# Local and strided attention into a routed FFN on one core: the routing sum a step later, row tiles a step or two earlier, buffer clearing and stores moved

## The chip, the cores and the metric

One core of one Trainium2 chip runs the whole program. The metric is the device time of one execution in microseconds. The median of three runs before the change is 591.56 us (589.87, 591.56 and 591.76).

## What is computed

Attention over 8 batches and 8 heads of 576 tokens with 64 features: the first four heads look back at most 31 tokens (Local), the other four at the tokens with the same position modulo 32 (Strided). The result, 4608 rows of 512 values, goes through a mixture of experts: every token is sent to the best of 8 experts, two matrix products with a ReLU between, scaled by the gate's probability.

```python
# attention, per batch and head
scores = scale * q @ k.T
mask = (rel >= 0) & (rel < 32)  if h < 4 else  (rel >= 0) & (key % 32 == query % 32)
attn = softmax(where(mask, scores, -1e9))
x[:, h*64:(h+1)*64] = attn @ v            # x: 4608 x 512

# mixture of experts
logits = x @ w_gate + modality_bias[modality_id]
e_idx  = argmax(logits, axis=1)
gate_w = softmax(logits)[e_idx]           # sum of exponents plus 1e-9
for e in range(8):
    t = e_idx == e
    out[t] = gate_w[t] * (relu(x[t] @ w1[e]) @ w2[e])
```

## The kernel before

The 8 batches are taken as 4 pairs. A pair has 8 units, four of two Local heads and four of two Strided heads in turn, 32 units in all. One loop runs over the units; each turn of it (a step) holds the scores s of a unit (L349), the turned exponents t (L219), the values o (L386) of an earlier unit, for the strided ones ss (L444), ts (L219) and ot (L494). This order on TensorE is written out by hand. VectorE, ScalarE and GpSimd get their order from a scheduler that keeps dependencies and a priority by position in the program; SP's queue is in the order of the program, with the loads of later units and stores between.

A strided unit's exponents are spread over four offsets by a masked multiply into the tile eb: two on VectorE (L479), two on ScalarE (L483). exs (L458, L459) are exponents before the division, enp (L465) after it.

When a pair ends (ends maps the number of its last unit to its buffers; three steps later), a generator finish_pair begins, which is advanced by one yield at each step. It transposes the pair's features: row tiles xs (strided features, from the buffers xcs to the rows xt, four transposes and one ScalarE copy, L511) and column tiles xl (L518), stores the rows xt to DRAM (xd), multiplies the gate (lg, ls) and then advances another generator, route, by its yields:
- lt turns the logits; lo is the logits less their maximum, its exponent is taken on ScalarE (L631); oh is the one-hot expert, cum its running count (L637).
- waits[1] steps later: sml, the sum of the exponents (L641, L642) and its reciprocal in val (L643), put behind the last enp (L465, list spots) by an ordering dependency without a wait (behind_units); then new, fst, stp and cnt (L645 to L651), the counts before each pair.
- waits[2] steps later: rk and po, the place of a token in its expert, cut into pos, paf and pbf; one-hots ha and hb (L672); hv (L681, GpSimd), the token and gate value times hb; waits[3] steps later the matmul en (L687), which turns the table ent and is stored to the list ld.
- tabulate, from the second pair on: the matmul ct (L735) sums cnt over the partitions, cts copies it, and a chain on VectorE (L746 to L836) makes the table of which expert fills which of 12 slots of 384 tokens.

The stores of the rows are not issued at once, but put on a list and issued one by one, some per step, by the table SPREAD; GpSimd issues those of pairs 0 and 1 (L581), SP those of pair 2 (L577), ScalarE those of pair 3 (L577). Three buffers raw for weights (1 MB each) are loaded on GpSimd by indirect DMA (L904); the third of them shares its memory with the rows of pair 2, and its load waits until their stores have landed. fx buffers (tokens gathered, L872) are cleared by ScalarE (L870) before the first gathers, in the first microseconds.

The FFN runs over the 12 slots: for each of 8 blocks 12 matmuls h (L1036) and 9 matmuls o (L1050), with weights split into a high and a low part by ScalarE (wh, L1071) and VectorE (wl, L1072), hh (L1039) and hl the split of h. Between, as far as it goes, stand the last steps of pair 3: its column and row tiles and its routing.

Of the kernel before, what the change touches and what calls it, by code (L numbers as in the profile page):

```python
# [11 lines left out]
F32 = mybir.dt.float32  # L12
# [8 lines left out]
P = 128  # L21
# [25 lines left out]
EARLY, BEGIN, HOLD = 3, 28, 26  # L47
SPREAD = 1, 2, 1, 0, 1, 1, 2, 1
ROWS = 32, 24
# [137 lines left out]
def attention_moe(ctx: ExitStack, tc: tile.TileContext, a, out):  # L187
# [7 lines left out]
    def pa(name):  # L195
        return ps.tile([P, 512], F32, tag="a", name=name)
# [64 lines left out]

    spots, exps = [], []

# [140 lines left out]
    class Strided:  # L404
# [63 lines left out]
        def turn(self):  # L468
            n, r0 = self.n, ROWS[self.n % 2]
            kn = r0 + 72  # L470
            tp = pa(f"ts{n}").rearrange("p (g q) -> p g q", g=4)
            for g in range(4):
                c0 = 32 + 72 * g
                self.point = turned_to(tp[0:kn, g, :], self.en[:, c0 - r0:c0 + 72])
            self.eb = eb = lp.tile([104, 8, 4, 36], F32, tag="eb", name=f"eb{n}")
            src = tp[0:kn].rearrange("p g (j x) -> p (g j) x", j=2)[:, :, 0:36]
            sh = [kn, 8, 2, 36]
            c0 = C_T + 4 * (n % 2)
            nc.vector.tensor_tensor(  # L479
                eb[0:kn, :, 0:2, :], src.unsqueeze(2).to_broadcast(sh),  # L480
                cf[0:kn, c0:c0 + 2].unsqueeze(1).unsqueeze(3).to_broadcast(sh), ALU.mult)
            for t in (2, 3):
                nc.scalar.activation(eb[0:kn, :, t, :], src, AF.Copy, scale=cf[0:kn, c0 + t:c0 + t + 1])  # L483

        def values(self):
            n, eb, vs, b = self.n, self.eb, vsp[self.n % 2], self.b
            kn = ROWS[n % 2] + 72
            for g2 in range(2):
# [13 lines left out]
                mark(nc.scalar.copy(dst, ot.rearrange("p (r q) -> p r q", r=16)))  # L502

    def finish_pair(bp, xt, xcs):

        def rows_of(c, k0):
            kn = min(4, 9 - k0)
            t = pa(f"xs{bp}{c}{k0}").rearrange("p (g q) -> p g q", g=4)
            for k in range(kn):
                turned_to(t[:, k, :], xcs[2 + c][:, P * (k0 + k):P * (k0 + k + 1)])  # L510
            nc.scalar.copy(xt[:, k0:k0 + kn, 256 + P * c:256 + P * c + P], t[:, :kn, :])  # L511

# [10 lines left out]

        if bp < EARLY:
            routing = route(bp, xt, xcs, (0, 1, 1, 1))
            next(routing)
            for c in range(2):
                rows_of(c, 0)
                columns_of(c, 0)
# [32 lines left out]
        next(routing)  # L562
        for k0 in (0, 4, 8):
            for c in range(2):
                next(routing, None)
                yield
                rows_of(c, k0)
            store_rows(bp, xt, k0, min(4, 9 - k0), nc.scalar)
        yield from routing
# [13 lines left out]
    def route(bp, xt, xcs, waits=(LT, RS, RK - RS, LW)):  # L583
# [56 lines left out]
        sm = ap.tile([P, 9], F32, tag="sml", name=f"sml{bp}")  # L640
        behind_units(nc.vector.tensor_reduce(sm[:], lo[:], AX.X, ALU.add))  # L641
        nc.vector.tensor_scalar(sm[:], sm[:], 1e-9, None, ALU.add)  # L642
# [27 lines left out]
        def hot(n, base, at, name, dt):  # L670
# [5 lines left out]

        ha = hot(LA, LA * bp, pa_f, "ha", F32)
        hb = hot(LB, 0, pb_f, "hb", BF16)
        hv = ap.tile([P, 9, 2, LB], F32, tag="hv", bufs=1, name=f"hv{bp}")
        sh = [P, 9, 2, LB]  # L680
        nc.gpsimd.tensor_tensor(  # L681
            hv[:], hb.unsqueeze(2).to_broadcast(sh), val.unsqueeze(3).to_broadcast(sh), ALU.mult)
        for _ in range(waits[3]):
            yield
# [179 lines left out]
    def token_parts(n, le, xrows):  # L864
# [3 lines left out]
        if n.startswith("0_"):  # L868
            for h in range(TH):
                nc.scalar.copy(xt[:, h, :], idle[:])  # L870
        for h in range(TH):
# [316 lines left out]
    for n in range(nu + 3):  # L1188
# [30 lines left out]
        if n + 2 < nu:  # L1219
            units[n + 2].prep()  # L1220
        ready = len(stores) if n >= HOLD else 9
        pop(POPS if n == nu + 2 else 1)
        for _ in range(min(ready, SPREAD[(n - 2) % 8])):
# [78 lines left out]
```

## Time and profile before

| | us |
|---|---|
| median of three runs | 591.56 |
| range of the runs | 589.87 to 591.76 |
| the profiled execution | 586.73 |
| span of it, first to last instruction | 584.7 |
| TensorE (PE) busy | 567.4 |
| VectorE (DVE) busy | 385.8 |
| ScalarE (ACT) busy | 331.4 |
| GpSimd (POOL) busy | 204.5 |

The attention phase lasts until about 150 us, the FFN from there to the end. PE is the queue of matmuls; idle time of the other engines counts only where PE waits for them. A row of the timeline gives the start in microseconds after the first instruction, the length, the engine, the line, the operation and its tiles, and in brackets how long the engine had stood still before and what ended that. Rows of one line that follow each other are drawn together (x64).

### The profile page before, as it was taken

Reading aid. Unit: us, or ns where it says so; the run is one execution under the profiler, and the core shown is the slowest. Engines: PE = TensorE matmul, PEld = TensorE weight load, DVE = VectorE, ACT = ScalarE, POOL = GpSimd, SP = SyncE. Lnnn points to the kernel's source line nnn. Section 1 sums busy time; section 2 is a strip of 40 time slices with the busy share of each in tenths; the row PEclk is TensorE's granted clock in tenths of the full one; section 3 lists DMA queues with packets and bytes.
Section 4 is the critical chain, followed back from the end, with each engine's and each line's share of the span. In section 5 each row is a group of like instructions: output and inputs, shape, how many; then the busy total and the mean of one; then the engine's idle time right before and its main releaser. Section 6 shows DMA issues by size and latency. Waiting matters only on the chain.

```text
span 584.7 us, 13778 instructions
## 1 busy us (share of the span) xinstructions
PE 567.4 (97%) x5449; PEld 500.9 (86%) x5449; DVE 385.8 (66%) x927; ACT 331.4 (57%) x662; POOL 204.5 (35%) x204
## 2 busy tenths in 40 slices
PE   9989999998999999999999999999999999999995
PEld 5878888777788899989999999989999998999984
DVE  6885977978866794676674756666574767664431
ACT  7789888787744454555453545545464455545342
POOL 3011021214257307444464335554433434423020
PEclk9999999999999999999999999999999999999998
DMA  8988889977796407766543275231413166323421
GB/s 274 342 283 267 296 289 302 307 253 233 259 357 222 191 1 242 248 200 223 150 161 73 80 208 198 59 83 63 91 54 81 50 219 201 112 42 126 145 103 46
DMA packets 63277, 104.31 MB, mean 178 GB/s; under 512 B 37027, under 2 KB 37539, under 8 KB 59108
## 3 DMA queue, kind: packets, MB, share of 16 engines
q0 software_dynamic: 16032, 57.47, 28.4%
q1 hardware_dynamic: 45636, 43.29, 25.4%
q10 hardware_dynamic: 1536, 2.58, 1.3%
q8 instruction: 45, 0.74, 0.5%
q14 instruction: 28, 0.23, 0.1%
HBM read 98.29 MB, written 19.18 MB: 201 GB/s over the span
## 4 chain that ended last, share of the span: by engine, by line
PE 86%; ACT 5%; DVE 5%; issue 3%; POOL 0%; DMA 0%; POOLq 0%; ACTq 0%; DVEq 0%
PE h L1036 35%; PE o L1050 34%; PE s L349 2%; PE ss L444 2%; PE o L386 2%; PE lg L589 1%; ACT et L373 1%; PE warm L207 1%; PE xl L219 1%; PE ot L494 1%; ACT xc L502 1%; PE t L219 1%; PE ts L219 1%; PE xs L219 1%; PE xt L219 1%
## 5 line engine op out<-in xcount | busy, mean ns | idle before, releaser
L1072 DVE TENSOR_TENSOR wl<-raw,wh 128x512 fp32r<-128x512 f32 x192 | 124.9, 688 | 83.8 <-ACT wh L1071 81.9
L1071 ACT CAST wh<-raw 128x512 fp32r<-128x512 f32 x192 | 109.7, 619 | 116.3 <-PE o L1050 110.3
L1036 PE MATMUL h<-xh,wl 128*128 128x384 f32 x384 | 129.7, 338 | 0.0
L1036 PE MATMUL h<-xl,wh 128*128 128x384 f32 x384 | 129.2, 336 | 0.0
L1036 PE MATMUL h<-xh,wh 128*128 128x384 f32 x384 | 128.1, 337 | 0.0
L1050 PE MATMUL o<-wl,hh 128*128 128x512 f32 x288 | 113.8, 395 | 0.0
L1050 PE MATMUL o<-wh,hl 128*128 128x512 f32 x288 | 113.7, 395 | 0.0
L1050 PE MATMUL o<-wh,hh 128*128 128x512 f32 x288 | 112.6, 391 | 0.0
L1039 ACT ACTIVATE hh<-h 128x384 fp32r<-128x384 f32 x96 | 47.2, 491 | 84.8 <-PE h L1036 84.3
L1041 DVE SCALAR_TENSOR_TENSOR hl<-h,hh 128x384 fp32r<-128x384 f32 x96 | 53.4, 556 | 55.4 <-ACT hh L1039 55.2
L904 POOL DMA_INDIRECT raw<-in_w,wi x48 | 55.8, 1162 | 83.2 <-ACT hh L1039 61.3
L1036 PEld LDWEIGHTS h<-xh,wh 128*128 128x128 f32 x384 | 72.2, 188 | 4.4 <-PE h L1036 0.4
L1036 PEld LDWEIGHTS h<-xl,wh 128*128 128x128 f32 x384 | 72.1, 188 | 4.0 <-issue 0.8
L1036 PEld LDWEIGHTS h<-xh,wl 128*128 128x128 f32 x384 | 72.0, 188 | 0.2 <-issue 0.2
L872 POOL DMA_INDIRECT fx<-xd,le x36 | 41.8, 1162 | 84.0 <-DMA work<-work 31.5
L1050 PEld LDWEIGHTS o<-wh,hl 128*128 128x128 f32 x288 | 54.0, 188 | 11.4
L1050 PEld LDWEIGHTS o<-wl,hh 128*128 128x128 f32 x288 | 54.0, 188 | 9.2
L1050 PEld LDWEIGHTS o<-wh,hh 128*128 128x128 f32 x288 | 54.1, 188 | 8.9
L889 POOL DMA_INDIRECT le<-ld,li x36 | 40.1, 1113 | 43.2 <-DVE li L811 15.8
L1058 POOL DMA_INDIRECT out<-y,le x36 | 37.0, 1027 | 38.5 <-ACT y L1057 34.5
L581 POOL DMA_DIRECT2D xd<-xt x18 | 10.0, 560 | 67.4 <-ACT xt L511 27.8
L999 DVE COPY work<-fx 128x1536 uint16<-128x1536 uint16 x18 | 30.7, 1745 | 3.1 <-DMA fx<-xd,le 3.1
(197 smaller groups left out, 768.7 us busy)
## 6 DMA issues: line engine op xcount, KB each, us to landing
vv<-in_vl SPq DMA_DIRECT2D x32, 292.5 KB, 4.4
qks<-in_qks SPq DMA_DIRECT2D x32, 288.0 KB, 4.6
qk<-in_qkl SPq DMA_DIRECT2D x16, 304.0 KB
qk<-in_qkl SPq DMA_DIRECT2D x16, 288.0 KB, 4.6
xd<-xt POOLq DMA_DIRECT2D x18, 256.0 KB, 5.1
vsp<-in_vs SPq DMA_DIRECT2D x16, 256.0 KB, 5.8
xd<-xt SPq DMA_DIRECT2D x9, 256.0 KB
xd<-xt ACTq DMA_DIRECT2D x2, 1024.0 KB, 6.6
```

Source lines behind the costliest of these rows:

```text
L219: return nc.tensor.transpose(dst, src, ident)
L872: ins = in_turn(nc.gpsimd.indirect_dma_start(xt[:, h, :], None, xd[0:xrows, :], IOA(ap=le[:, h, 0:1], axis=0), **bounds))
L889: in_turn(nc.gpsimd.indirect_dma_start(le[:, h, :], None, ld[0:1 + last, :], IOA(ap=li[:, s, h:h + 1], axis=0)))
L904: ins = nc.gpsimd.indirect_dma_start(raws[j].rearrange("p f c -> p (f c)"), None, a["w"], IOA(ap=wi[:, s, j:j + 1], axis=0), bounds_check= ...
L999: pin(nc.vector.tensor_copy(rows[:, :, w, :], halves(xt)[:, :, :, w]))
L1036: nc.tensor.matmul(hp, w[:, a1], x[:, c, :], start=(k == 0), stop=(k == 11))
L1039: steps.append(nc.scalar.activation(hh[:], hp, AF.Relu))
L1041: nc.vector.scalar_tensor_tensor(hl[:], hp, 0.0, hh.bitcast(F32), ALU.max, ALU.subtract)
L1050: nc.tensor.matmul(os[h], hx[:, m], w[:, 512:1024], start=(f == 0 and i == 0), stop=(f == 7 and i == 2))
L1058: outs.add(in_turn(nc.gpsimd.indirect_dma_start(out, IOA(ap=le[:, h, 0:1], axis=0), y[:], None, bounds_check=NT - 1, oob_is_err=False), True))
L1071: nc.scalar.copy(wh[:, c], raw[:, c])
L1072: nc.vector.tensor_tensor(wl[:, c], raw[:, c], wh[:, c].bitcast(F32), ALU.subtract)
```

## The change

- SPREAD, the table of stores per step, becomes 1, 2, 1, 0, 1, 2, 1, 1: the last entries are exchanged, so one store goes a step earlier.
- route is given (0, 2, 0, 1) steps for the first three pairs in place of (0, 1, 1, 1): sml, new, fst, stp and cnt come a step later, in the same step as rk; and sml is ordered behind the last masked multiply L479 (list ebs) instead of behind the last enp (list spots).
- turn_rows is rows_of moved out of finish_pair. The first row tile of each of the two feature blocks is done by the loop, one and two steps after the step of the pair's last unit; finish_pair begins three steps after it; for pair 3 this takes them out of the FFN's entry.
- In route, hb and hv stand ahead of ha in the program.
- The clearing copies of fx are tied to the last marked copy of the attention (pace), so that they come late in the attention phase, not at its start.
- Pair 3's rows are stored by SP's queue; the first store is issued when its generator starts.

```diff
-SPREAD = 1, 2, 1, 0, 1, 1, 2, 1
+SPREAD = 1, 2, 1, 0, 1, 2, 1, 1
...
-            nc.vector.tensor_tensor(
+            ebs.append(nc.vector.tensor_tensor(
                 eb[0:kn, :, 0:2, :], src.unsqueeze(2).to_broadcast(sh),
-                cf[0:kn, c0:c0 + 2].unsqueeze(1).unsqueeze(3).to_broadcast(sh), ALU.mult)
+                cf[0:kn, c0:c0 + 2].unsqueeze(1).unsqueeze(3).to_broadcast(sh), ALU.mult))
...
+    def turn_rows(bp, xt, xcs, c, k0):
+        kn = min(4, 9 - k0)
+        t = pa(f"xs{bp}{c}{k0}").rearrange("p (g q) -> p g q", g=4)
+        for k in range(kn):
+            turned_to(t[:, k, :], xcs[2 + c][:, P * (k0 + k):P * (k0 + k + 1)])
+        nc.scalar.copy(xt[:, k0:k0 + kn, 256 + P * c:256 + P * c + P], t[:, :kn, :])
...
-            routing = route(bp, xt, xcs, (0, 1, 1, 1))
+            routing = route(bp, xt, xcs, (0, 2, 0, 1))
             next(routing)
             for c in range(2):
-                rows_of(c, 0)
                 columns_of(c, 0)
...
-        for k0 in (0, 4, 8):
+        store_rows(bp, xt, 0, 4, nc.sync)
+        for k0 in (4, 8):
             for c in range(2):
                 next(routing, None)
                 yield
                 rows_of(c, k0)
-            store_rows(bp, xt, k0, min(4, 9 - k0), nc.scalar)
+            store_rows(bp, xt, k0, min(4, 9 - k0), nc.sync)
...
-        behind_units(nc.vector.tensor_reduce(sm[:], lo[:], AX.X, ALU.add))
+        behind_units(nc.vector.tensor_reduce(sm[:], lo[:], AX.X, ALU.add), ebs)
...
-        ha = hot(LA, LA * bp, pa_f, "ha", F32)
         hb = hot(LB, 0, pb_f, "hb", BF16)
...
         nc.gpsimd.tensor_tensor(
             hv[:], hb.unsqueeze(2).to_broadcast(sh), val.unsqueeze(3).to_broadcast(sh), ALU.mult)
+        ha = hot(LA, LA * bp, pa_f, "ha", F32)
...
-            nc.scalar.copy(xt[:, h, :], idle[:])
+            after_landing(nc.scalar.copy(xt[:, h, :], idle[:]), pace[-1])
...
+        if n - 1 in ends or n - 2 in ends:
+            turn_rows(*ends[n - 1 if n - 1 in ends else n - 2], 0 if n - 1 in ends else 1, 0)
```

On VectorE, in the routing of pair 1 as the units of pair 2 begin, the order before is this; sml and cnt are of the routing, mxs, eb and exs of a strided unit.

```order
L645 TENSOR_TENSOR new_2165<-cum_2086,ohb_2081 128x8
L646 TENSOR_TENSOR fst<-new_2165,cnt 128x8
L456 TENSOR_REDUCE mxs_2217<-ss_2136 128x16
L648 TENSOR_TENSOR stp<-fst 128x8
L651 TENSOR_TENSOR cnt<-cum_2086,fst 128x8
L641 TENSOR_REDUCE sml_2161<-lo_2068 128x9
L479 TENSOR_TENSOR eb_2233<-ts_2228,cf_sb 104x8x72
L458 TENSOR_TENSOR exs_2219<-ss_2136,mxs_2217 128x288
L642 TENSOR_SCALAR sml_2161<-sml_2161 128x9
```

In the same place the order after has eb first, and the counts are gone from here.

```order
L638 SCALAR_TENSOR_TENSOR cum_2086<-ohb_2081 128x72
L456 TENSOR_REDUCE mxs_2208<-ss_2136 128x16
L479 TENSOR_TENSOR eb_2224<-ts_2219,cf_sb 104x8x72
L642 TENSOR_REDUCE sml_2265<-lo_2068 128x9
L458 TENSOR_TENSOR exs_2210<-ss_2136,mxs_2208 128x288
```

The counts now stand some twenty operations further on, mixed with the last steps of the routing and with mx, ex and qd of a local unit. These are rows of the order after.

```order
L465 TENSOR_TENSOR enp_112<-exs_2210,sms_2213 128x288
L646 TENSOR_TENSOR new_2269<-cum_2086,ohb_2081 128x8
L669 SCALAR_TENSOR_TENSOR pbf_2287<-paf_2285,pos_2279 128x9
L673 TENSOR_TENSOR ha_2293<-cf_sb,paf_2285 128x324
L356 TENSOR_REDUCE mx_2299<-s_2232 128x5
L647 TENSOR_TENSOR fst<-new_2269,cnt 128x8
L673 TENSOR_TENSOR hb_2289<-cf_sb,pbf_2287 128x288
L359 TENSOR_TENSOR ex_2300<-s_2232,mx_2299 128x320
L330 COPY qd_102<-qk_2174 64x18x32
L649 TENSOR_TENSOR stp<-fst 128x8
L652 TENSOR_TENSOR cnt<-cum_2086,fst 128x8
L747 TENSOR_SCALAR ni_2377<-cts_2373 128x8
```

cnt, which stood ahead of sml, is now the last before ni, the first operation of the slot table.

On TensorE the matmul ct, which reads cnt and stp, stands in that step between the strided values ot and the strided scores ss; this is the order before.

```order
L494 MATMUL ot_2340<-eb_2233,vsp_113 64x72 x8
L494 MATMUL ot_2350<-eb_2233,vsp_113 64x72 x8
L735 LDWEIGHTS cb_sb
L735 MATMUL ct_2363<-cnt,cb_sb 128x16
L735 LDWEIGHTS cb_sb
L735 MATMUL ct_2363<-stp,cb_sb 128x16
L444 MATMUL ss_2338<-qks_2094,qz_104 36x18 x32
L219 MATMUL ts_2438<-cf_sb,enp_112 96x128 x4
L338 LDWEIGHTS cb_sb
L338 MATMUL s_2449<-cb_sb 128x256
```

In the order after a row tile xs stands ahead of it.

```order
L494 MATMUL ot_2341<-eb_2224,vsp_113 64x72 x8
L494 MATMUL ot_2351<-eb_2224,vsp_113 64x72 x8
L219 MATMUL xs_2364<-cf_sb,xc_136 128x128 x4
L736 LDWEIGHTS cb_sb
L736 MATMUL ct_2370<-cnt,cb_sb 128x16
L736 LDWEIGHTS cb_sb
L736 MATMUL ct_2370<-stp,cb_sb 128x16
L444 MATMUL ss_2339<-qks_2094,qz_104 36x18 x32
L219 MATMUL ts_2444<-cf_sb,enp_112 96x128 x4
L338 LDWEIGHTS cb_sb
```

The four transposes of xs have come in between; what comes behind ct is the same.

On ScalarE at the FFN's entry, the casts wh of the weights, the copies of column and row tiles (xc, xt) and the split hh of the first block stand like this before; wh_04 is the first to read the third weight buffer.

```order
L1071 CAST wh_02_3523<-raw_3157 128x512
L518 COPY xc_140<-xl_3431 128x512
L1071 CAST wh_02_3523<-raw_3157 128x512
L518 COPY xc_140<-xl_3437 128x128
L1071 CAST wh_03_3590<-raw_3157 128x512 x2
L511 COPY xt_138<-xs_3463 128x4x128
L1039 ACTIVATE hh_00_3427<-h_00_3414 128x384
L511 COPY xt_138<-xs_3501 128x4x128
L1071 CAST wh_04_3626<-raw_3224 128x512 x2
L577 DMA xd<-xt_138 128x4x512
L597 COPY ls_3461<-lg_3440 128x384
```

After, hh of the first block stands behind the casts of wh_04.

```order
L1072 CAST wh_02_3530<-raw_3158 128x512 x2
L1072 CAST wh_03_3590<-raw_3158 128x512 x2
L519 COPY xc_140<-xl_3443 128x512
L519 COPY xc_140<-xl_3449 128x128
L1072 CAST wh_04_3626<-raw_3230 128x512 x2
L1040 ACTIVATE hh_00_3439<-h_00_3426 128x384
L509 COPY xt_138<-xs_3476 128x4x128
```

The store of rows has left this queue.

## Rows read from the trace of the kernel before

**Rows 1.** The page: busy time, share of the span, instructions

```profile
span 584.7 us, 13778 instructions
PE 567.4 (97%) x5449; PEld 500.9 (86%) x5449; DVE 385.8 (66%) x927; ACT 331.4 (57%) x662; POOL 204.5 (35%) x204
```

**Rows 2.** Windows: length, busy of PE, PEld, DVE, ACT, POOL; clock, DMA share, GB/s

```profile
66.00:84.00 18.00, 16.49 (x402) 14.21 (x398) 14.19 (x54) 14.75 (x36) 4.08 (x7) 1.00 0.92 313
100.00:122.00 22.00, 19.54 (x492) 16.89 (x489) 19.95 (x100) 18.44 (x43) 4.09 (x7) 1.00 0.86 280
134.00:165.00 31.00, 29.00 (x406) 23.69 (x402) 25.51 (x111) 22.80 (x54) 12.59 (x13) 0.94 0.77 265
165.00:570.00 405.00, 405.00 (x2075) 366.79 (x2074) 252.70 (x430) 195.05 (x353) 168.13 (x150) 1.00 0.45 140
```

**Rows 3.** Timeline of PE: start, length, line, tiles, [idle before <-releaser], attention's end steps

```profile
41.46 0.34 PE L349 MATMUL s<-qk,qd 128*64 128x64 f32 x4 [2.00 <-issue]
...
106.77 0.18 PE L735 MATMUL ct<-cnt,cb_sb 128*128 128x16 bf16 x1
...
111.95 1.20 PE L687 MATMUL en<-hv,ha 128*36 128x64 f32 x18 [0.51 <-POOL hv L681]
...
116.62 0.66 PE L219 MATMUL xs<-cf_sb,xc 128*128 128x128 f32 x4 [0.43 <-ACT et L373]
...
119.99 0.25 PE L444 MATMUL ss<-qks,qz 128*36 128x18 f32 x5 [1.09 <-issue]
...
141.79 1.22 PE L494 MATMUL ot<-eb,vsp 104*64 104x72 f32 x32 [1.14 <-ACT eb L483]
...
144.01 0.63 PE L219 MATMUL ts<-cf_sb,enp 128*96 128x128 f32 x2 [0.86 <-DVE pbf L668]
```

**Rows 4.** Waits over the whole span: total, times, longest

```profile
DVE sml L641 <- ACT lo L631: 3.1, 3, 1.2
```

**Rows 5.** Timeline of DVE, the second pair's routing

```profile
101.80 0.16 DVE L651 TENSOR_TENSOR cnt<-cum,fst 128x8 bf16<-128x8 bf16 x1
103.12 0.23 DVE L641 TENSOR_REDUCE sml<-lo 128x9 f32<-128x72 f32 x1 [1.17 <-ACT lo L631]
103.26 0.75 DVE L479 TENSOR_TENSOR eb<-ts,cf_sb 104x576 f32<-104x576 f32 x1
...
107.72 0.46 DVE L465 TENSOR_TENSOR enp<-exs,sms 128x288 f32<-128x288 f32 x1
...
110.28 0.17 DVE L746 TENSOR_SCALAR ni<-cts 128x8 int32<-128x8 f32 x1
```

**Rows 6.** Timeline of ACT, the second and third pair's routing

```profile
102.81 0.27 ACT L631 ACTIVATE lo<-lo 128x72 f32<-128x72 f32 x1
...
134.80 1.19 ACT L373 COPY et<-t 64x512 f32<-64x512 f32 x2 [0.88 <-PE t L219]
...
140.85 0.89 ACT L483 ACTIVATE eb<-ts,cf_sb 104x288 f32<-104x288 f32 x2 [1.35 <-DVE eb L479]
```

**Rows 7.** Timeline of POOL: two stores, the value table, the third weight load

```profile
73.62 1.07 POOL L581 DMA_DIRECT2D xd<-xt  x2 [2.25 <-ACT xc L502]
74.70 1.17 POOL L681 TENSOR_TENSOR hv<-hb,val 128x576 f32<-128x576 bf16 x1
...
156.30 1.10 POOL L904 DMA_INDIRECT raw<-in_w,wi  x1 [9.29 <-ACT xc L518]
```

**Rows 8.** Timeline of ACT at the start: the clearing casts

```profile
2.56 3.20 ACT L870 CAST fx<-idle 128x512 f32<-128x512 bf16 x6
...
8.84 0.42 ACT L360 ACTIVATE ex<-ex 128x256 f32<-128x256 f32 x1 [1.81 <-DVE ex L359]
```

**Rows 9.** Timeline of ACT at the entry of the FFN

```profile
158.29 0.55 ACT L1039 ACTIVATE hh<-h 128x384 fp32r<-128x384 f32 x1
...
162.19 0.62 ACT L1071 CAST wh<-raw 128x512 fp32r<-128x512 f32 x1 [2.88 <-DMA raw<-in_w,wi]
```

**Rows 10.** Windows of 1 us, columns as in rows 2

```profile
144.00:145.00 1.00, 0.98 (x4) 0.63 (x4) 0.50 (x3) 0.83 (x3) 0.69 (x2) 0.50 1.03 405
```

More of the change, by code (lines that the diff above doesn't have):

```diff
@@ L260, in attention_moe @@
     stp = cp.tile([P, NBP, E], BF16, name="stp")
-    spots, exps = [], []
+    spots, exps, ebs = [], [], []
     def behind_units(ins, of=None):
@@ L502, in values @@
                 mark(nc.scalar.copy(dst, ot.rearrange("p (r q) -> p r q", r=16)))
-    def finish_pair(bp, xt, xcs):
[L506 to L511, printed above, removed]
+    def turn_rows(bp, xt, xcs, c, k0):
[4 more added lines that the diff above has]
+        nc.scalar.copy(xt[:, k0:k0 + kn, 256 + P * c:256 + P * c + P], t[:, :kn, :])
+    def finish_pair(bp, xt, xcs):
+        rows_of = partial(turn_rows, bp, xt, xcs)
         def columns_of(c, k0):
```

## The prediction, made before the changed kernel ran

> **What bounds the kernel now.** I read the page first: TensorE is busy for 567.4 of 584.7 us [rows 1], so no other engine is a bound on the whole, and a change can only bring back TensorE's idle time, or the time in which its clock is low, or add to these. The windows then say where that is. From 165 to 570 us TensorE is busy in all of 405.00 us [rows 2], and the change touches nothing there. Its idle time lies in the attention phase: 1.51 us in 66 to 84, 2.46 us in 100 to 122, 2.00 us in 134 to 165 (length less busy, [rows 2]); the last of these stretches also has a mean clock of 0.94 where the others have 1.00. The timeline of TensorE names what each gap waits for [rows 3]: the value table hv (0.51), a row tile's bank (0.43), the strided exponents eb (1.14), the chain behind pbf (0.86), and two gaps of 2.00 and 1.09 us that wait for nothing the profile shows. Last come the timelines of the engines that feed it. VectorE stands still in front of the routing sum sml, 3.1 us in three times [rows 4], and the next pair's masked-exponent multiply eb, and with it ScalarE's half of the same tile, stands behind it [rows 5, 6].
>
> A difference of 0.3% (1.8 us) is about what a measurement of this kernel can tell from none. The profiled execution took 586.73 us, 2.03 more than its span, and lies 4.83 below the median of the three runs, 591.56. I work out a difference against the profiled execution and lay it on the median.
>
> **The end of pair 0 (34 to 46 us).** Two row tiles of four transposes each (0.66 us, the length of the xs row in [rows 3], an upper bound since the next matmuls begin before its end) move from the pair's last step to one and two steps earlier. PE's work is the same; only what falls into idle time is gained. The first of them stands in front of the strided scores, the second in front of the local ones, in whose middle lies the 2.00 us gap [rows 3]. If that gap begins when it began, work ahead of it fills it; if it moves with the instructions, nothing is won. Bounds 0 and -1.3, I take **-0.6**.
>
> **Pair 0's routing under pair 1's end (66 to 84 us).** In the order after, eb runs before sml, during the time VectorE stood still, and sml follows when lo is there. The row of pair 1's routing shows the size: sml waits 1.17 us until ScalarE ends lo at 103.08 (102.81 + 0.27), and eb (0.75) comes after it [rows 5, 6]. So everything behind eb gains about 0.7; the exponents' subtraction exs still waits for sml. Further, hv on GpSimd stands behind two store issues, 1.07 us for both [rows 7]; with the new spread of stores one is left, and hv begins about 0.5 earlier, which closes the gap before en. All of this stretch's idle time is 1.51, and no more can be had. VectorE is nearly full here in steps, so the whole can't be counted on. Bounds -0.4 (the store alone) and -1.5, I take **-1.2**.
>
> **Pair 1's routing under pair 2 (100 to 122 us).** The same gain of 0.7 begins this stretch, but here a wait comes in that the kernel before doesn't have. The count matmul ct reads cnt. Before, cnt is done at 101.96 (101.80 + 0.16) while sml waits anyway, and ct runs at 106.77 without waiting [rows 3, 5]. Now new, fst, stp and cnt come behind the masked multiply enp, mixed with six operations (pbf, ha, mx, hb, ex, qd) which before fill the 2.56 us from enp's start at 107.72 to ni's at 110.28 [rows 5]. Four more small operations at a spacing of about 0.1 put cnt's end at 110.28 + 0.4, less 0.7 for the earlier eb: about 110.0. TensorE reaches ct at 106.77 + 0.66 for the row tile that now stands in front of it, 107.43, so it stands still for about 2.6 us; queued behind ct on its engine are the strided scores, enp's transposes, the outputs and the next scores, all of pair 2. Two waits further on are swallowed: 0.51 before en and 0.43 before a row tile [rows 3]. That leaves +1.6. Below, the 1.09 gap could be swallowed as well, and VectorE could drain half a microsecond sooner: 0. Above, +2.6, if none of the waits is. VectorE is the engine that decides, and it is busy for 19.95 of 22.00 us here [rows 2], so I stay with the working: **+1.5**.
>
> **Pair 2's routing and the entry of the FFN (134 to 165 us).** eb gains as before; ScalarE then sets ot's wait, because three clearing casts of 0.53 (3.20 / 6, [rows 8]) now stand in front of its et copies. 0.88 of their 1.6 us falls in ScalarE's idle time at 134.80, the rest in the 1.35 it waits at 140.85 [rows 6]. The 1.14 gap at ot shrinks to about 0.4. Then ct waits for cnt behind enp as above; since pbf, which TensorE waited for until 144.01 [rows 3], is just ahead of cnt on VectorE, ts moves by only +0.2. The first row tile falls in that wait and the second lands in the stretch that it was already in; taken out of the FFN's entry, the first is worth -0.5. What is open is the clock. After 1.14 and 0.86 us of idle time with 1.2 us of work between, it stands at 0.50 [rows 10]; a mean of 0.94 over 31 us is 0.06 x 31 / 0.5 = 3.7 us at half, 1.9 us of full-speed work lost [rows 2]. The two waits get somewhat shorter together (0.4 and about 1.3, in place of 2.00), so I count a quarter of this, -0.5. Sum of the stretch **-0.8**, bounds -2.5 (no fall of the clock) and +1.5 (the rival on the third weight load, below).
>
> By the Trainium skill (TensorE: Matmul & The Clock Gate, section "What's actually happening"), "the default state is throttled, and activity releases the throttle". This agrees with the 0.50 behind the two waits in [rows 10], and the 1.09 us gap in a stretch at 1.00 [rows 2, 3] shows that not every wait costs the clock; taken strictly, for any wait above that, the rule would make the ct wait of pair 1 cost the clock too, and that is the second rival.
>
> **What costs nothing.** The clearing casts at the start leave a ScalarE that, 2 us on, waits 1.81 us for VectorE [rows 8]: 0. One-hot hb ahead of ha in the code doesn't turn the two round on VectorE, where ha still comes first: 0 beyond the small move that I counted with hv. Pair 3's stores go to SP's queue and leave ScalarE's; they run earlier, beside a DMA that is busy for 0.77 of the stretch [rows 2], and nothing that TensorE wants is queued behind them on SP: 0, bounds -0.3 and +0.5. The masked exponents' spread on SP puts two stores instead of one ahead of the last unit's strided values; 0, and +0.5 if a store's rows are late.
>
> By the Trainium skill (DMA: Bandwidth & Descriptors, section "Issuing engines are not separate DMA queues"), a transfer issued from another engine runs on the same 16 DMA engines and saves only issue time. That speaks against a gain from the stores' new queue, and no run here shows it yet; the sum is the same with it, and the rival below on the third weight load would be the likelier for it.
>
> **Sum.** -0.6 - 1.2 + 1.5 - 0.8 = -1.1: 585.6 for a profiled execution, **590.5** on the median, -0.2%.
>
> **Rivals.**
> *The gains come whole and ct's wait is short.* For it: the wait in front of sml is real in three places, and each small operation behind enp is only 0.1 to 0.2 us. Against it: eight operations stand between enp and the end of cnt, and TensorE has nothing else queued. With -0.9, -1.5, +0.4 and -1.7 (no fall of the clock behind pair 2) the sum is -3.7: 587.9.
> *The ct wait costs the clock (the slower side).* A wait of 2.6 us in one piece in front of ct is longer than the 2.00 us in two that came before the clock of 0.50 [rows 3, 10]. If the clock falls there too, 1.9 us of work is lost, and with VectorE late the term is +2.6 in place of +1.5: -1.1 + 1.9 + 1.1 = +1.9, 593.5. It decides from where ct waits for more than about 2 us. Against it: the single wait of 2.00 us at 41.46 [rows 3] lies among work that went on as before.
> *The third weight load lands late.* Before, its issue on GpSimd waits 9.29 us, to 156.30 [rows 7], for pair 2's stores to land (it shares their buffer), and ScalarE has its data at 162.19; the first hh was done by then, at 158.29 [rows 9]. In the order after, the first hh stands behind the two casts of that load, so it can't start before it lands. With the same landing, hh0 would begin at about 163.4, five us later, and the first o group, due at about 165, slips by an estimated 0.7. For each microsecond by which it lands later, TensorE loses one. Against it: the stores are one fewer at the end, and should land earlier. With a landing 3 us later: -1.1 + 0.7 + 3 = +2.6, 594.2.
> *The change does nothing*, since DMA is nearly full (0.92 and 0.86 of the time, [rows 2]) and the loads set the pace: 0, 591.6. This is within the forecast's class.
>
> **How the numbers follow.** The sum, with the last rival in its class: 0.46, all of it within 0.3%. Whole gains: 0.34, faster. Clock: 0.14, slower. Third load: 0.06, slower. So faster by over 0.3% 0.34, within 0.3% 0.46, slower 0.20. The range of the forecast alone is 589.3 to 592.5, the sum with half of each bound. To hold eight in ten it must take in most of the whole gains and a part of the clock's case: 587.6 to 593.6.
>
> **What would show each step.** Right: VectorE's wait at sml under 0.9 us or gone in favour of a wait at exs, eb ahead of it, and TensorE's 1.14 gap at ot cut to under 0.5; a wait at ct of 2 to 3 us in pair 1 with cnt as its releaser; the gap before en gone in both pairs; a mean clock in 134 to 165 about as before. Wrong: ct not waiting (then the whole gains), a granted clock of 0.50 at 107 to 114 (then the second rival), hh0 later than 163 with TensorE waiting for it (the third), or a difference that arises behind 165, of which I know no reason.

## The result and the profile after

| | us |
|---|---|
| before, median of four runs | 590.71 |
| after, median of four runs (594.93 to 595.11) | 595.04 |
| ratio, 95% interval | 1.0074, 1.0049 to 1.0099 |
| profiled execution after, span | 595.11, 593.2 |

The change makes the kernel slower by 0.74%, some 4.3 us. The two profiled executions differ by 8.4 us, about twice that. The first one of before was short: a second trace of the same kernel, taken later, has 591.67 us and a span of 589.7. So size is read from the timed runs, and the place from the traces.

The windows of the kernel after (the columns of [rows 2]):

```profile
66.00:84.00 18.00, 17.32 (x398) 14.79 (x394) 15.56 (x54) 15.05 (x34) 4.17 (x7) 1.00 0.94 312
...
100.00:122.00 22.00, 17.96 (x394) 15.48 (x392) 18.73 (x94) 13.46 (x34) 4.22 (x7) 0.84 0.78 253
...
134.00:165.00 31.00, 26.74 (x432) 22.32 (x432) 25.13 (x116) 22.94 (x53) 10.22 (x11) 0.94 0.75 242
...
200.00:570.00 370.00, 370.00 (x1884) 335.44 (x1883) 232.42 (x379) 178.01 (x317) 144.46 (x130) 1.00 0.44 133
```

The same windows of the second trace of the kernel before:

```profile
66.00:84.00 18.00, 16.48 (x402) 14.20 (x399) 14.38 (x53) 14.73 (x36) 4.08 (x7) 1.00 0.92 312
100.00:122.00 22.00, 21.02 (x491) 17.98 (x486) 20.29 (x103) 18.48 (x44) 4.08 (x7) 1.00 0.88 300
134.00:165.00 31.00, 26.24 (x397) 20.49 (x394) 25.49 (x114) 21.97 (x52) 12.78 (x13) 1.00 0.72 247
```

From 200 to 570 us nothing has changed (all of 370.00 busy, as before). In 66 to 84 TensorE's idle time is 0.68 us where [rows 2] gave 1.51. The loss is in 100 to 122: 4.04 us idle (22.00 less 17.96) against 2.46 and 0.98 in the two traces before, and the mean clock is 0.84 where it was 1.00. In 134 to 165 it is 4.26 us, against 2.00 and 4.76; here the kernel before varies as much as the change does.

The timeline of TensorE after, beside [rows 3]:

```profile
105.26 0.66 PE L219 MATMUL xs<-cf_sb,xc 128*128 128x128 f32 x4
109.64 0.20 PE L736 MATMUL ct<-cnt,cb_sb 128*128 128x16 bf16 x1 [3.73 <-DVE cnt L652]
...
109.79 2.12 PE L444 MATMUL ss<-qks,qz 128*36 128x18 f32 x64
...
116.80 1.17 PE L688 MATMUL en<-hv,ha 128*36 128x64 f32 x18
...
147.94 0.66 PE L219 MATMUL xs<-cf_sb,xc 128*128 128x128 f32 x4
151.07 0.19 PE L736 MATMUL ct<-cnt,cb_sb 128*128 128x24 bf16 x1 [2.48 <-DVE hb L673]
```

ct, which didn't wait before, waits 3.73 us in pair 1, and 2.48 us in pair 2 (there the profile names hb; cnt is the second operation behind it on VectorE and ends 0.17 later, at 151.01). TensorE comes to it at 105.91 (109.64 less 3.73), 0.86 ahead of its time before, and to en at 116.80, 4.85 behind. The scores ss take 2.12 us behind the wait. In the trace of the kernel before they took 1.30:

```profile
107.07 1.30 PE L444 MATMUL ss<-qks,qz 128*36 128x18 f32 x64
```

The clock says why (windows of 1 us of the kernel after):

```profile
108.00:109.00 1.00, 0.00 (x0) 0.00 (x0) 1.00 (x2) 0.95 (x4) 0.98 (x2) 0.50 1.02 397
...
113.00:114.00 1.00, 1.00 (x14) 0.66 (x14) 1.00 (x3) 0.63 (x2) 0.00 (x0) 0.50 0.86 285
114.00:115.00 1.00, 1.00 (x30) 1.00 (x26) 0.99 (x7) 0.97 (x3) 0.00 (x0) 0.68 0.63 150
```

It is at 0.50 while TensorE still stands, and through the work behind the wait until 114.

VectorE and GpSimd in the same place, beside [rows 5] and [rows 7] (timelines, first VectorE, then GpSimd):

```profile
101.61 0.23 DVE L642 TENSOR_REDUCE sml<-lo 128x9 f32<-128x72 f32 x1 [0.80 <-ACT lo L632]
...
105.55 0.46 DVE L465 TENSOR_TENSOR enp<-exs,sms 128x288 f32<-128x288 f32 x1
...
107.73 0.45 DVE L330 COPY qd<-qk 64x576 f32<-64x576 f32 x1
108.09 1.41 DVE L649 TENSOR_TENSOR stp<-fst 128x8 bf16<-128x8 bf16 x1
109.43 0.15 DVE L652 TENSOR_TENSOR cnt<-cum,fst 128x8 bf16<-128x8 bf16 x1
```

```profile
104.73 1.07 POOL L582 DMA_DIRECT2D xd<-xt  x2 [2.65 <-DVE xt L399]
107.62 0.67 POOL L582 DMA_DIRECT2D xd<-xt  x1 [1.82 <-DVE hb L673]
108.31 1.17 POOL L681 TENSOR_TENSOR hv<-hb,val 128x576 f32<-128x576 bf16 x1
```

sml still waits 0.80 us, but eb no longer stands behind it. cnt is the last of the operations behind enp, and one of them, stp, takes 1.41 us. It runs beside hv on GpSimd and ends at 109.50, when hv does (108.31 + 1.17). In the trace of the kernel before it took 0.15:

```profile
101.73 0.15 DVE L648 TENSOR_TENSOR stp<-fst 128x8 bf16<-128x8 bf16 x1
```

### The profile page after: what moved, and what is told of

Read it like the earlier page. It is cut to its first block, busy times and chain, and to the rows that moved or that the text cites. A ratio compares the mean times of both kernels' runs of the same rounds, so it can differ in the third digit from the quotient of the medians.

```text
span 593.2 us, 13778 instructions
## 1 busy us (share of the span) xinstructions
PE 571.2 (96%) x5449; PEld 503.4 (85%) x5449; DVE 389.4 (66%) x927; ACT 331.2 (56%) x662; POOL 201.7 (34%) x204
## 4 chain that ended last, share of the span: by engine, by line
PE 80%; DVE 8%; issue 6%; ACT 3%; another core or an unknown queue 1%; POOL 0%; POOLq 0%; ACTq 0%
PE h L1037 33%; PE o L1051 32%; PE ss L444 2%; PE s L349 2%; PE o L386 2%; PE ot L494 1%; PE warm L207 1%; PE t L219 1%; PE lg L590 1%; DVE xt L399 1%; PE ts L219 1%; DVE mx L356 1%; PE xs L219 1%; PE xl L219 1%
## 5 line engine op out<-in xcount | busy, mean ns | idle before, releaser
L873 POOL DMA_INDIRECT fx<-xd,le x36 | 37.9, 1052 | 83.2 <-DMA work<-work 31.5
```

The lines of the kernel that those rows point to most:

```text
L873: ins = in_turn(nc.gpsimd.indirect_dma_start(xt[:, h, :], None, xd[0:xrows, :], IOA(ap=le[:, h, 0:1], axis=0), **bounds))
```

## The experiments

Two theories stood against each other. **A**: the counts stand behind the masked multiply enp on VectorE, ct on TensorE waits for them with all of pair 2 queued behind, and the clock falls. **B**: the row tiles, the clears or the stores cost the time. The kernels were timed in four groups, each on a chip of its own, with the kernel before beside them. Its median was 590.74 us in the first group (the first three kernels of the table), 591.29 in the second (the old table of stores, counts behind eb, ct a step later, row tiles alone), 585.92 in the third (the three with 583 to 586 us) and 589.92 in the fourth (the matmuls and the two repeated), so I compare ratios; times in an expectation are those of an earlier group or of the result.

| kernel | median us | ratio to before, 95% |
|---|---|---|
| counts a step earlier | 588.23 | 0.9962, 0.9933 to 0.9991 |
| the sum's edit alone | 597.65 | 1.0129, 1.0090 to 1.0168 |
| all but the sum's edit | 588.87 | 0.9966, 0.9938 to 0.9995 |
| the old table of stores | 593.05 | 1.0048, 1.0017 to 1.0079 |
| counts ordered behind eb | 587.10 | 0.9943, 0.9903 to 0.9983 |
| the same, again | 587.82 | 0.9972, 0.9944 to 1.0001 |
| ct a step later in pair 1 | 590.15 | 0.9975, 0.9952 to 0.9999 |
| row tiles alone | 589.64 | 0.9969, 0.9948 to 0.9990 |
| behind eb, stores on ScalarE's queue | 583.45 | 0.9951, 0.9932 to 0.9970 |
| behind eb, clears at the start | 583.79 | 0.9963, 0.9935 to 0.9991 |
| sum and counts behind eb, alone | 586.34 | 1.0019, 0.9990 to 1.0047 |
| matmuls in ct's wait | 591.17 | 1.0022, 0.9997 to 1.0047 |
| the change, again | 593.77 | 1.0075, 1.0051 to 1.0100 |

**A second trace of the kernel before.**

> The kernel before, unchanged, for a second trace. The first profiled execution (586.73 us) lies 2.7 to 5 us under the four timed runs (589.42 to 591.76). If those differ by where the clock falls or by waits in the attention phase, a profiled execution of about 590 shows 3 to 4 us more idle time or half-clock time there, and none behind 165 us. If the first trace is the usual course, this one has its gaps (sums of TensorE idle: 1.5 us in 66 to 84, 2.5 in 100 to 122, 2.0 in 134 to 165) within 0.5 us.

591.67 us. Its windows stand above. Idle time in 100 to 122 is less than in the first trace, in 134 to 165 it is 2.8 us more, for the most part because ot waits 1.6 for eb in place of 1.14, and h waits 1.6 for wh, which it didn't in the first. The entry of the FFN is where these two traces of the kernel before differ most; its time varies from 587.55 to 594.97 in 19 runs on this chip. Part of the expectation missed: 1.5 us more is idle behind 165 too, nearly all of it in one wait of h for xl (1.4, at 188.20).

**The counts put back.**

```diff
-        for _ in range(waits[1]):
+        for w in range(waits[1]):
             yield
+            if bp < EARLY and w == 0:
+                counts()
```

> The changed kernel, with new, fst, stp and cnt put back to one step before the routing sum (as in the kernel before), everything else as changed. Theory A (the count matmul ct waits for cnt behind the masked multiply, and the clock falls after the wait): ct does not wait in either pair, the half clock at 108 to 114 us is gone, and the time is 6 to 9 us under the changed kernel's 595.04, that is 586 to 589, under the kernel before by 2 to 4 us. Theory B (the row tiles, clears and stores cost the time): within 1.5 us of 595.04.

588.23 us, 0.38% under the kernel before. ct doesn't wait, and the clock in 100 to 122 is 1.00. Theory A holds, B is out.

**The sum's edit alone**, in the kernel before (waits 0, 2, 0, 1; sml behind ebs).

> The kernel before with one edit: the routing sum and the counts a step later, behind the masked multiply (waits 0, 2, 0, 1). Theory A: ct waits 2 us or more in pairs 1 and 2, the clock falls, and the time is 3 to 6 us over the kernel before. Theory B: not slower than the kernel before, since eb gains its 0.7 us three times and nothing of the rest is changed: 0 to -2 us.

597.65 us, 1.29% over: this edit alone costs more than the whole change, and at 6.9 us more than the 3 to 6 expected of theory A. The mean clock is 0.84 in 100 to 122 and 0.90 in 134 to 165. Waits of TensorE in it (total, times, longest):

```profile
PE ct L735 <- DVE hb L672: 3.1, 1, 3.1
PE ct L735 <- DVE cnt L651: 3.0, 1, 3.0
```

**All but the sum's edit.**

```diff
-            routing = route(bp, xt, xcs, (0, 2, 0, 1))
+            routing = route(bp, xt, xcs, (0, 1, 1, 1))
...
-        behind_units(nc.vector.tensor_reduce(sm[:], lo[:], AX.X, ALU.add), ebs)
+        behind_units(nc.vector.tensor_reduce(sm[:], lo[:], AX.X, ALU.add))
```

> The changed kernel with the routing sum as before (waits 0, 1, 1, 1, behind the last enp), so the row tiles, the spread of stores, the clears, the one-hot order and pair 3's stores alone. Theory A: no wait at ct, the waits of VectorE in front of the sum (about 1 us, three times) are back, the time is 0 to 2.5 us under the kernel before. Theory B: over it by 3 us or more.

588.87 us, 0.34% under, with no wait at ct; VectorE waits 3.2 us in front of sml again. The two halves (+1.29% and -0.34%) make +0.95%, against +0.74 measured for the whole.

**The old table of stores**, to part hv from stp.

```diff
-SPREAD = 1, 2, 1, 0, 1, 2, 1, 1
+SPREAD = 1, 2, 1, 0, 1, 1, 2, 1
```

> The changed kernel with the table of stores as before, so that GpSimd's value table hv again stands behind two stores instead of one and begins about 0.5 us later. In the changed kernel one operation of VectorE that meets hv takes 1.41 us in place of 0.15 (cnt in pair 0's routing, stp in pair 1's, ni in pair 2's), and stp's length is part of the 3.73 us that ct waits. Theory of the collision: with hv later stp is over before hv begins, takes 0.15, ct waits about 2.4 us in pair 1, and the time is 1 to 3 us under 595.04 (the clock may not fall then). Rival (stp's length has another cause, say the bf16 form): stp stays at 1.4 and ct at 3.7, the time within 1 us of 595.04.

The timelines of VectorE, GpSimd and TensorE in that kernel:

```profile
106.49 0.15 DVE L649 TENSOR_TENSOR stp<-fst 128x8 bf16<-128x8 bf16 x1
106.57 0.15 DVE L652 TENSOR_TENSOR cnt<-cum,fst 128x8 bf16<-128x8 bf16 x1
...
107.24 1.17 POOL L681 TENSOR_TENSOR hv<-hb,val 128x576 f32<-128x576 bf16 x1
...
106.78 0.19 PE L736 MATMUL ct<-cnt,cb_sb 128*128 128x16 bf16 x1 [2.46 <-DVE cnt L652]
```

stp is over before hv begins and takes 0.15; ct waits 2.46 us in place of 3.73. The time is 1.0048 of before in place of 1.0074, which the intervals don't part for sure. The clock still falls (0.84 in 100 to 122), which the expectation had left open.

**The counts in their new step, but behind eb.**

```diff
-        behind_units(nc.vector.tensor_tensor(new[:], cum[:, :, 0], ohb[:, :, 0], ALU.subtract))
+        behind_units(nc.vector.tensor_tensor(new[:], cum[:, :, 0], ohb[:, :, 0], ALU.subtract), ebs)
```

> The changed kernel with one word more: the counts new, fst, stp and cnt keep their new step, but are ordered behind the masked multiply of exponents eb like the routing sum, not behind the masked multiply enp. If it is the place behind enp that costs, and not the step, ct doesn't wait (cnt ends about 3 us earlier), and the time is that of the kernel with the counts put back, 588.2, within 1 us. If a step later is itself too late, ct waits over 1 us and the time lies above 590.5.

587.1 us, the fastest against before. So it is not the step, but the word behind which the scheduler puts the counts. Later it was run beside the changed kernel, on one chip.

> The changed kernel with the counts behind eb, a second time, beside the changed kernel: 0.4 to 0.8 per cent under the kernel before, 6 to 9 us under the changed one; no wait at ct.

587.82 against 593.77 for the change and 589.92 for the kernel before. TensorE there passes from the row tile to ct without a wait (timeline):

```profile
103.67 0.66 PE L219 MATMUL xs<-cf_sb,xc 128*128 128x128 f32 x4
104.16 0.17 PE L736 MATMUL ct<-cnt,cb_sb 128*128 128x16 bf16 x1
```

This version beats both, by 6 us and, with an interval that just reaches 1, by 2 us. The gain expected over before, 0.4 to 0.8%, came as 0.57 and 0.28; the 5.95 us under the change lie just short of the 6 to 9 expected. What it meets next, from the waits of TensorE in its first trace:

```profile
PE ts L219 <- DVE enp L465: 1.5, 1, 1.5
PE h L1037 <- ACT wh L1072: 1.2, 1, 1.2
```

enp now ends last in pair 2, and at the FFN's entry ScalarE waits for the first weights to land.

**ct a step later in pair 1.**

```diff
-            if bp < EARLY - 2:
+            if bp < EARLY - 1:
                 yield
```

> The changed kernel with the counts as late as in it, but pair 1's count matmul ct (and its slot table and its value matmul en) one step later on TensorE; pair 2's are as in the changed kernel. If the loss in pair 1 is only that TensorE stands at ct with all its work behind it, the 3.73 us wait and the half clock at 108 to 114 go, and the time falls by 3.5 to 5.5 us to 589.5 to 591.5; pair 2's 2.48 us wait and its half clock stay. If VectorE's chain is late for other reasons too (exs, enp), TensorE waits at ss or ts in its place by over 2 us.

590.15 us, and 0.25% under before: TensorE no longer pays for the late counts of pair 1 when it has other work ahead of ct. The timeline of TensorE:

```profile
111.83 0.17 PE L736 MATMUL ct<-cnt,cb_sb 128*128 128x16 bf16 x1
...
114.99 1.22 PE L494 MATMUL ot<-eb,vsp 96*64 96x72 f32 x32 [0.63 <-DVE xt L399]
```

ct at 111.83 doesn't wait, though cnt ends just before (111.78); ot waits 0.63 and the column tiles xl 0.53. The clock in 100 to 122 is 1.00. The wait in pair 2 is left (2.5 us), and with it the clock of 0.50 behind it; the kernel is 3 us over the one with the counts behind eb on the same chip, which is about what pair 2 costs, though the intervals of the two overlap.

**Row tiles alone**, in the kernel before (turn_rows as in the change, pair 3's stores on ScalarE's queue).

> The kernel before with one edit: the first row tiles one and two steps after the pair's last unit, pair 3's included (its first store then goes out on ScalarE's queue when its steps start). If the row tiles bring the 1.9 us that the rest of the change brought without the routing sum, the time is 1 to 2.5 us under the kernel before. If the gain is the stores' queue, the clears or the one-hot order, it lies within 0.8 us of the kernel before.

589.64 us, 0.31% under: as much as the rest of the change brings (0.34%), within their intervals.

**The stores' queue, and the clears**, each put back in the kernel with the counts behind eb.

> The changed kernel with the counts behind eb (the run before with 587.1 us), and pair 3's stores on ScalarE's queue as before, the first at the start of pair 3's steps. There the first weights wh waited for the raw weights until 150.34 us, and the matmul h 1.2 us for wh; the gain of 5.4 us that stood at 125 us had shrunk to 0.3 at the first logits of pair 3. If the early stores on SP's queue take bandwidth from the weight loads (1 MB each, 9 us from issue to landing), the first raw lands earlier without them on SP, h waits under 0.5 us and the time is 1 to 2.5 us lower, 584.6 to 586. If the queue is nothing (same 16 DMA engines, same moment), within 1 us of 587.1.

> The changed kernel with the counts behind eb, and the six clearing casts at the start as before. If the late clears cost (1.6 us each on ScalarE at about 134 and 153 us, in front of et and of the weight casts), the time is 1 to 2 us lower than 587.1 and wh is ahead. If taking them away from the start is worth something (the traces of kernels without them there show 0.6 to 1.3 us less at the first ss), it is 0.5 to 1.3 us higher. If both are hidden, within 0.5 us.

0.9951 and 0.9963, between the two runs of the kernel they start from (0.9943 and 0.9972): neither can be told from nothing. In both traces TensorE has no wait of h for wh (it was 1.2 us), so also in the one that keeps the stores on SP's queue; what took the wait away, the queue, the clears or the other chip, isn't shown.

**Sum and counts behind eb, alone**, in the kernel before.

> The kernel before with the routing sum and the counts a step later, both behind the masked multiply of exponents eb: the edit of the sum alone (597.65 us), without its side effect on the counts. If the sum's move is worth what the wait in front of it says (about 0.7 us in three places, with all of it on TensorE's path), 1 to 2.5 us under the kernel before. If VectorE's standing there was off the path, since TensorE waits for others by then, within 0.8 us of it. Either way 6 us or more under 597.65, if only the place of the counts cost the time.

586.34 us, 1.0019 of before: the move of the routing sum, freed of its side effect, brings nothing that can be measured. Timelines of TensorE and VectorE, and of TensorE in the kernel before:

```profile
66.67 0.69 PE L386 MATMUL o<-vv,et 128*64 128x65 f32 x16 [0.32 <-ACT xt L511]
...
69.48 1.22 PE L494 MATMUL ot<-eb,vsp 104*64 104x72 f32 x32
...
66.99 0.23 DVE L641 TENSOR_REDUCE sml<-lo 128x9 f32<-128x72 f32 x1 [0.82 <-ACT lo L631]
```

```profile
66.80 0.69 PE L386 MATMUL o<-vv,et 128*64 128x65 f32 x16 [0.32 <-ACT xt L511]
...
69.61 1.22 PE L494 MATMUL ot<-eb,vsp 104*64 104x72 f32 x32
```

eb is done before sml, which waits 0.82, and TensorE comes to ot at 69.48, 0.13 from before, as far as it was off at o already. eb wasn't what it waited for there.

**Matmuls in ct's wait**, to part the wait from the clock: 12 and 8 products of zeros, whose result is thrown away.

```diff
+        for _ in range((12, 8, 0)[ph]):
+            nc.tensor.matmul(tb, idle[:, 0:P], idle[:], start=True, stop=True)
```

> The changed kernel with matmuls on a tile of zeros put into the bank of ct ahead of it, 12 in pair 1 and 8 in pair 2 (about 0.2 us each at the full clock, 2.6 and 1.7 us), which fill most of the time that TensorE waits for cnt (3.73 and 2.48 us). They are thrown away by ct's own start. The wait itself stays. If the half clock behind the waits (6.4 us in pair 1, 3.7 in pair 2) is a cost of its own, it is gone and the time falls by 2.5 to 4.5 us against the changed kernel on the same chip. If what comes behind waits for other engines anyway, within 1 us of it.

> The changed kernel as it is, beside the other two of this call: over the kernel before by 0.5 to 1.0 per cent, with both waits at ct (about 3.7 and 2.5 us) and the half clock behind both.

Timeline of TensorE in the kernel with these matmuls, then its windows, then the same windows of the changed kernel on that chip:

```profile
104.34 2.75 PE L736 MATMUL ct<-idle 128*128 128x512 bf16 x12
108.23 0.17 PE L739 MATMUL ct<-cnt,cb_sb 128*128 128x16 bf16 x1 [1.13 <-DVE cnt L652]
...
108.35 1.30 PE L444 MATMUL ss<-qks,qz 128*36 128x18 f32 x64
```

```profile
100.00:122.00 22.00, 20.87 (x440) 17.18 (x442) 20.66 (x103) 16.95 (x40) 4.18 (x7) 1.00 0.84 274
134.00:165.00 31.00, 27.62 (x392) 21.34 (x390) 24.29 (x108) 22.96 (x54) 12.25 (x12) 1.00 0.77 258
```

```profile
100.00:122.00 22.00, 17.58 (x394) 15.05 (x394) 18.58 (x95) 13.53 (x34) 4.21 (x7) 0.92 0.78 252
134.00:165.00 31.00, 26.77 (x430) 21.86 (x428) 25.07 (x117) 23.08 (x54) 11.14 (x12) 0.94 0.76 247
```

TensorE is held for as long (2.75 and 1.13 us), but the clock stays at 1.00, and ss behind it takes 1.30 us and not 2.12. The time is 591.17 against 593.77. So of the 5.95 us between the change (593.77) and the version with the counts behind eb (587.82), the clock is 2.6 and the waits are 3.35, if the matmuls change nothing but the clock; the scatter of the eleven times of each kernel leaves one to two microseconds either way on each (an estimate).

## Why the prediction was wrong

**The forecast and the case that came.** I forecast 590.5 with a range to 593.6, and 595.04 came. The mechanism that decided it was in the prediction, as the rival "the ct wait costs the clock", 0.14 and 593.5; the forecast itself took a good third of the wait (0.94 of 2.6 us) as swallowed and the clock as safe.

**The step that failed: the clock, put at nothing in the term for pair 1's routing, +1.5.** The term was a wait of 2.6 us at ct, less what later waits swallow, at a full clock. What pair 1 costs can be read from the strided values ot in front of ct to those of the second strided unit behind it, the same instructions in every kernel. Timelines of TensorE, in pairs: the first trace of before, the change (again), the matmuls in ct's wait, the counts behind eb (again).

```profile
105.61 1.22 PE L494 MATMUL ot<-eb,vsp 104*64 104x72 f32 x32
125.46 1.22 PE L494 MATMUL ot<-eb,vsp 104*64 104x72 f32 x32
...
103.87 1.22 PE L494 MATMUL ot<-eb,vsp 104*64 104x72 f32 x32
128.34 1.22 PE L494 MATMUL ot<-eb,vsp 104*64 104x72 f32 x32
...
102.70 1.22 PE L494 MATMUL ot<-eb,vsp 104*64 104x72 f32 x32
123.88 1.22 PE L494 MATMUL ot<-eb,vsp 104*64 104x72 f32 x32
...
102.52 1.22 PE L494 MATMUL ot<-eb,vsp 104*64 104x72 f32 x32
121.94 1.22 PE L494 MATMUL ot<-eb,vsp 104*64 104x72 f32 x32
```

| kernel | from ot to ot, us |
|---|---|
| before, its two traces | 19.85, 19.12 |
| the change, its two traces | 24.49, 24.47 |
| matmuls in ct's wait | 21.18 |
| counts behind eb, again | 19.42 |

The change comes to the first of these ot ahead of the kernel before, as forecast, by 1.3 to 1.7 us. Then pair 1 costs 4.6 to 5.4 us in place of 1.5. Of the 5.05 us by which the change exceeds the kernel with the counts behind eb, 3.29 go when the clock is held at 1.00, and 1.76 are left for the wait. So the wait, less what was swallowed, has nearly the size of the term, and the clock came on top of it. These are single traces; the timed runs give 2.6 us for the clock in both pairs.

**Where the term was lucky.** The wait was well worked out as far as it went: enp was to begin 0.41 us before TensorE arrives (107.02, which is 107.72 less 0.7, against 107.43), and begins 0.36 before (105.55 against 105.91); with the old table of stores the wait is 2.46. In the change it is 3.73, because stp beside hv takes 1.26 us more, which I hadn't seen. But more was swallowed than the 0.94 I had set against it: beside the wait at ct only 0.31 us of idle time is left in 100 to 122 (4.04 less 3.73). The two misses nearly cancel. That cnt ended at 109.58, near the 110.0 of the working, is luck of the same kind: enp began 1.5 us earlier than reckoned, and from there to cnt's end it took 4.03 us in place of 2.96.

**The clock.** I left it out of the sum for pair 1, since a gap of 2.00 us at 41.46 had passed without harm. Both of ct's waits cost it, also the one of 2.46 us with the old table of stores. For both places together it is 2.6 us by the matmuls in the wait; I had priced one place at 1.9.

**Pair 2 and the FFN's entry, -0.8.** Mis-sized: ct waits 2.48 in place of 1.3, and the clock falls behind it. The clock's fall, which I had counted as nearly as before, happened in the first trace of before and not in its second.

**The gain for pair 0's routing, -1.2.** Wrong in its cause. With the sum's move alone TensorE isn't earlier; VectorE stood still in front of sml, but TensorE didn't wait for what came behind. Idle time of an engine that nobody waits for had been taken as a term of the sum. The gaps of that stretch did shrink (1.51 to 0.68), and to 0.26 with the row tiles alone. The earlier hv, counted as a gain of at least 0.4, met cnt there, which took 1.41 us. What the change gains ahead of pair 1 arises at the end of pair 0, from the row tiles. From the first strided values ot of the kernel to the fifth (starts at about 19 and 51 us) TensorE takes 32.70 and 32.51 us in the two traces of before, 32.65 with the sum's edit alone and 32.77 with sum and counts behind eb, but 31.25 with the row tiles alone and 31.29 and 31.11 in the change. From there to the ot in front of ct it takes 53.35 and 53.36 us before, and 54.04 and 53.10 in the change. So -0.6 was too small, -1.2 came as nothing that the two traces show, and that their sum of -1.8 is near what came is luck.

**What was right.** The row tiles as a gain (-0.6 at pair 0's end and -0.5 at the FFN's entry; alone 0.31%, some 1.8 us with an interval of 0.6 to 3.1), the clears, the one-hot order and the queue of the stores (together nothing that can be measured beside the row tiles), and that the third weight load doesn't decide: ScalarE waited for it until 168.80 in the trace after (1.45 us), and TensorE didn't wait for hh.

**Two slips of the working.** Half of the way to each bound gives 588.4 to 592.9 for the forecast alone, not 589.3 to 592.5; and the order after has nine operations between enp and cnt, not eight. Neither would have moved the outcome.

With the counts behind eb, part of the gain is lost at the FFN's entry, where h waits for the first weights; how much can't be said, because the kernel before itself varies by 2.8 us of idle time there between its two traces. Why it does, and what the gaps are that wait for nothing, stays open.

## What to carry to other kernels

When an operation is moved with a loosely ordered group behind it, look in the order at the last one of the group and at who reads it: here four operations of 0.15 us, put behind the wrong predecessor, cost 6 us, and one word gave them back. A wait on a hand-ordered TensorE queue is paid less the idle time that it swallows further on: the two waits at ct, 3.73 and 2.48 us, cost about 3.35 together. But both were paid a second time in the clock, 2.6 us, and a sum that leaves the clock out misses that. A stall of another engine counts only where TensorE is seen to wait for what stands behind it.

## What the runs showed of the hardware

Small VectorE operations on SBUF tensors that met GpSimd's elementwise operation hv were held until it ended: cnt, stp and ni took 1.41, 1.41 and 1.42 us beside hv (1.17 us) in the three routings of the trace after, and 0.15 or 0.17 elsewhere; with hv later, in the kernel with the old table of stores, stp was back at 0.15. It was so in the kernel before, too, where another operation met hv: ni at 111.39 took 0.54 us and ended with it. Operations that read a matmul's result weren't held: eb took 0.74 us beside the same hv (110.73 against 110.72). The Trainium skill (SBUF — State Buffer, section "Who interferes with whom") says that a VectorE instruction with two SBUF inputs contends with a GpSimd instruction that reads SBUF, and that the one that comes first blocks the other whole. The lengths agree: stp ends when hv does. For ni, an operation with a number, the same section names another way to contend, a mode that reads through both ports. By the starts in the rows stp (108.09) came ahead of hv (108.31) and yet was the one held, which the rows don't explain.

TensorE's clock was at 0.50 behind the waits of 3.73 and 2.48 us, and matmuls on zeros in the waits kept it at 1.00; these were worth 2.6 us. The length of one wait doesn't tell whether the clock falls: it stayed at 1.00 behind the 2.00 us at 41.46 in the kernel before, and was at 0.50 from 143 us in the kernel with the stores on ScalarE's queue, whose TensorE had waited 0.58 us for enp (to 140.98) and 1.31 us for a load (to 143.40) there.
